# A fused linear-attention and gated feed-forward kernel: last stores split by 64 rows, partial sums moved to another buffer, filler matmuls and a new order

## The chip, the cores and the metric

The kernel runs on one core of a Trainium2 chip. The metric is the device time of one execution in microseconds (us), median of several. A core has five engines that run on their own: TensorE (PE; its weight loads are listed as PEld), VectorE (DVE), ScalarE (ACT), GpSimd (POOL) and SyncE (SP), which here only issues transfers. Sixteen DMA engines move the data. The engines wait for each other through semaphores; each works through its own queue strictly in order.

## The reference

Four batches, eight heads of width 48 and 768 positions go through a linear attention with a decaying state. Its output, 3072 tokens of width 384, goes through a feed-forward layer of width 2048 whose gate is a cosine.

```python
for t in range(S):                      # attention, per batch and head
    cur = outer(u * k[t], v[t])
    y[t] = r[t] @ (state + cur)
    state = w * state + outer(k[t], v[t])
h = x @ w_in                            # x: (3072, 384), w_in: (384, 2048)
g = h * cos(h)
out = g @ w_out                         # w_out: (2048, 384)
```

The weights arrive in double precision. The kernel turns each into a high and a low single-precision part and multiplies three times (high by high, low by high, high by low).

## The kernel before, in words

**Attention.** The 3072 tokens are worked in 24 chunks of 128. The first eight ("early") chunks hold the first positions of each batch. They have to be done before the feed-forward layer can run without breaks. A chunk is loaded (k, r, v), transposed on PE, scaled by the decay on DVE (`rT`, `kT`, L982 and L1001), multiplied (L1065), masked (L1073), and multiplied again into `x` (L1087, L1100), which ACT and DVE split into `xh` and `xl`. The sixteen later chunks do the same in another layout (L1383, L1389, L1463) between the steps of the feed-forward layer.

**Feed-forward.** Six blocks of 512 tokens pass through 16 slices of `w_in` and `w_out`, which makes 96 steps. A step is nine matmuls "h" of 512 columns (L503), an elementwise chain that alternates between ACT and DVE (qi L519, rest L522, cosine L525, gate L1586, high part L1589, low part L1592) and nine matmuls "o" (L516), which add into three PSUM banks. Blocks 0 and 1 take turns: their slices come in the pieces 0 to 2, 2 to 5, 5 to 10 and 10 to 16, since the weights arrive while they work. At the end of each of their first three pieces the three banks are copied to SBUF (L1623) and stored to scratch memory `part_d`: the first piece by SP (L1631), the next two by GpSimd transfers that add to what is there (L1633). At the fourth piece the sums are loaded back (L1641) and added, and DVE turns each bank into the buffer `ot` (L1652), from which SP stores the block in 16 transfers (L1671). There is one `ot` buffer of 128 x 1536 numbers. The copies take a buffer of the ring `R_f`, six buffers of 128 x 512 that also hold the cosine's argument, the converted weights and part of each later chunk.

**The last block** multiplies the other way round (L509), so its four chunks come out with tokens on the partitions. Each is copied (L1702) to a buffer of `R_f` and stored (L1712), the first three by SP, the last one by ACT.

**The order.** Each operation has an entry in `DUES` (a due time) and some an entry in `HOLDS`. A planner in `Plan.one_pass` runs through them with costs (in `op(...)`) and with a time `lat` until a result can be used, picks on each engine what is ready and due first, chooses buffers from the rings and so writes the queues. Buffers and waits follow from that order. Before the first attention product on PE (`first_A`), the planner's gaps on PE are filled with matmuls on zeros (`warm_up`, L1730), one per 0.22 of planned gap.

```python
def st():
    (nc.scalar if last else nc.sync).dma_start(dst, ob())
op(ACT if last else SP, s + 2.5, 0.6, st, [oc], [ob], lat=2.5)
```

Of the kernel before, what the change touches and what calls it, by code (L numbers as in the profile page):

```python
# [9 lines left out]
F32 = mybir.dt.float32  # L10
# [32 lines left out]
    136758, -74847, -43844, -28732, 302616, -88975, -71328, 46773, 176240, 38114, 271897, 215557, 326974,  # L43
    108836, 53012, 131186, -161706, 278206, -84719, -293075, -54461, -7640, 283819, -85697, 225756, 5593,
    -186679, -10247, -73373, -28930, -162082, 217987, -259366, -177497, -84941, -159201, -82184, -80393, -43863,
    -83055, -77972, 11589, -57274, -33785, -170957, -72005, 201058, -45669, 74469, -60635, 116586, -1076,
    111276, 75119, -54793, 79940, -38890, -89278, -125768, -238696, -60653, -52997, 21625, 301534, -101593,
    254771, -262222, -4970, -219414, 28091, -15110, -97894, -118263, 12053, -110128, 63549, 133177, 18614,
    -6951, 60025, -22060, -45024, -49677, 34204, 60125, -200205, -13302, -66174, -33036, -94433, -91164,
    -125037, -46149, -20654, -8595, 24466, -21539, 53811, 138429, 106136, -172876, 50367, -26165, 15995, 24273,  # L50
    -73113, -59577, 52435, -99831, 6426, -50099, 93499, -60680, -32457, -42871, 114144, 77795, 144490, 137391,
    58783, -23367, 58577, 208422, -111209, 186777, -11076, -42885, 38423, 100425, 7413, 63119, 35933, -82873,
    250196, 68613, 170627, 73983, 171298, 116684, 190202, 18014, 349844, 16050, 103196, -271912, -28477, 57946,
    290925, 2146, 33561, 87750, 82736, 172361, 96028, 40836, 105696, -9361, -144107, -33123, 99741, 1720,
    222152, -3585, 44166, 292726, 50264, -3417, 78702, 53863, 549, 113465, 8699, 37860, 176553, 165585, 100038,
    33248, -20572, -128785, 1518, 144259, 60247, 111734, -19349, 32045, 66708, -119633, -62142, 103845, 7872,
    221906, 105376, -223574, 64391, -119475, 99981, -10143, 69206, 82857, 22816, 161156, -2214, 80786, -18511,
    137292, 151469, 17062, -117219, 27894, 24386, 27670, 204170, 162618, 78171, 259079, 174814, 138450, 181046,
    10238, 112906, 347641, 318538, 211144, 102107, 153373, 148521, 132607, 118433, 89292, 171696, 128704,
    224680, 119833, 142656, 216497, 338377, 224213, 228681, 52471, 182421, 269447, -15748, 147984, 302852,  # L60
    286074, 34347, 185044, 298071, 23180, 78723, -179449, 119380, 127630, 4739, 200362, -47882, -78624, -67,
    101807, 208108, 151590, 281102, 33345, -24492, 84778, 189293, 149176, 299002, 138086, 120838, 117666,
    211708, 219288, 158855, 153765, 181158, 156137, 207030, 225525, 219795, 263347, 151158, 256475, 125769,
    109988, 90100, 99225, 182830, 149079, 210335, 235226, 217064, 109197, 158205, 373177, 166519, 231418,
    368046, 231808, 402665, 265446, 135760, 146596, 193207, 92655, 123719, 102006, 230749, 209030, 135713,
    186620, 213224, 193786, 310481, 321361, 240739, 159885, 356326, 109821, 206409, 160655, 36410, 117505,
    88418, 132605, 96715, 156058, 162907, 220231, 298782, 364481, 93736, 17158, 212980, -73432, 288595, 294841,
    296470, 172246, 66723, 372492, 296138, 168690, 134186, 224480, 266863, 261899, 191662, -237199, 374999,
    -8877, 107834, 204368, 189738, 236846, 275244, 395143, 104624, 363087, 387425, 335888, 381053, 217061,
    412705, 377859, 323997, 156149, 261201, 425835, 270672, 337145, 263398, 149282, 222003, 244052, 247831,  # L70
    248047, 247831, 214675, 320956, 240127, 336022, 244681, 246600, 428199, 207444, 245430, 210426, 250803,
    241749, 251901, 251612, 251612, 248581, 253162, 253162, 251012, 251312, 251312, 251962, 252712, 254012,
    258703, 259383, 259740, 261940, 264140, 265440, 267940, 269380, 270240, 267980, 268840, 269340, 270590,
    273560, 274810, 275560, 275560, 271840, 277110, 277110, 274960, 275260, 275260, 275910, 276660, 277960,
    285405, 286085, 271217, 273417, 275617, 276917, 282935, 284375, 285235, 282975, 283835, 280817, 285585,
# [191 lines left out]
    0.8, 1256: 0.1, 1258: 0.2, 1259: 0.8, 1260: 0.8, 1262: 0.8, 1263: 0.3, 1264: 0.2, 1265: 0.3, 1267: 0.5,  # L267
    1268: 0.2, 1269: 0.2, 1270: 0.2, 1272: 0.8, 1273: 0.3, 1274: 0.8, 1275: 0.8, 1277: 0.3, 1278: 0.5, 1280:
    0.2, 1281: 0.2, 1282: 0.3, 1284: 0.1, 1286: 0.2, 1287: 0.3, 1289: 0.2, 1290: 0.2, 1294: 0.5, 1297: 0.8,
    1299: 0.1, 1304: 0.5, 1308: 0.2, 1310: 0.1, 1317: 0.1, 1318: 0.1,  # L270
}


# [1610 lines left out]
```

## Time and profile before

| | us |
|---|---|
| median of 3 runs | 506.78 (506.75 to 508.08) |
| the profiled execution, its own time | 507.42 |
| its span (first to last instruction) | 505.6 |
| PE busy | 475.6 (94%) |
| DVE busy | 370.3 (73%) |
| ACT busy | 292.2 (58%) |
| GpSimd busy | 222.2 (44%) |
| mean granted TensorE clock | 0.981 |

The span is the part of an execution that the rows cover; 1.82 us of the profiled execution lie around it. Matmuls overlap and their ends are modelled, so that a PE that is busy in a whole stretch has no wait in it, and no more can be read from its share.

### The profile page before, as it was taken

What the parts mean: (1) busy time and instruction counts of PE and PEld (TensorE: products, weight loads), DVE (VectorE), ACT (ScalarE), POOL (GpSimd) and SP (SyncE); (2) the same over time, 40 slices, a digit from 0 to 9 for tenths busy, and PEclk for the clock granted to TensorE, in tenths of its full rate; (3) what the DMA queues carried; (4) which work ended last, traced back from release to release, by engine and by line L of the source; (5) the groups of instructions that cost most, each with busy time, mean ns of one, the idle gap of its engine ahead of it and who ended that gap; (6) DMA issues with size and microseconds to landing.
All of it is one profiled execution on the core that took longest, in us unless ns stands there. A gap on an engine that the chain in (4) does not pass through costs nothing.

```text
span 505.6 us, 11867 instructions
## 1 busy us (share of the span) xinstructions
PE 475.6 (94%) x4475; PEld 391.7 (77%) x4475; DVE 370.3 (73%) x686; ACT 292.2 (58%) x652; POOL 222.2 (44%) x225
## 2 busy tenths in 40 slices
PE   7999999999899999999999999999999999999940
PEld 6787788777678887688888888888888888899940
DVE  7899997998978967877787777678677557444430
ACT  5897876786765464465656555556555544444420
POOL 7674357746655874644484541574524200000000
PEclk9899999999999999999999999999999999999985
DMA  8774668869277565676873473766373300200001
GB/s 160 141 177 127 202 178 189 153 170 211 89 171 178 99 129 143 140 167 168 185 180 84 102 176 109 169 137 149 100 164 99 100 1 10 55 1 0 1 26 40
DMA packets 142538, 61.69 MB, mean 122 GB/s; under 512 B 122476, under 2 KB 135308, under 8 KB 142476
## 3 DMA queue, kind: packets, MB, share of 16 engines
q1 hardware_dynamic: 140554, 57.50, 46.4%
q0 software_dynamic: 1728, 3.15, 3.9%
q8 instruction: 36, 0.59, 0.5%
q10 hardware_dynamic: 194, 0.25, 0.1%
q14 instruction: 26, 0.21, 0.1%
HBM read 51.43 MB, written 9.44 MB: 120 GB/s over the span
## 4 chain that ended last, share of the span: by engine, by line
PE 75%; DVE 8%; DMA 5%; SPq 3%; ACT 2%; issue 1%; POOL 1%; DVEq 0%; ACTq 0%; POOLq 0%
PE bank L503 32%; PE bank L516 27%; PE bank L509 7%; PE bank L1383 3%; PE bank L1463 3%; DMA raw<-in_moe_w_out_dram 2%; DMA part<-f 1%; DVE f L864 1%; SPq L1671 1%; PE bank L973 1%; DVE f L876 1%; DVE A L1073 1%; DMA f<-part 1%; PE bank L1100 1%; ACT A L1038 1%
## 5 line engine op out<-in xcount | busy, mean ns | idle before, releaser
L503 PE MATMUL bank<-xh,w_in_hi 128*128 128x512 f32 x288 | 113.7, 395 | 1.8 <-DVE gl L1592 1.8
L503 PE MATMUL bank<-xh,w_in_lo 128*128 128x512 f32 x288 | 112.6, 391 | 1.2 <-DVE w_in_lo L888 1.2
L503 PE MATMUL bank<-xl,w_in_hi 128*128 128x512 f32 x288 | 112.4, 390 | 0.0
L519 ACT ACTIVATE qi<-bank 128x512 int32<-128x512 f32 (+1 forms) x102 | 58.0, 573 | 88.9 <-PE bank L503 83.7
L522 DVE SCALAR_TENSOR_TENSOR f<-bank,qi 128x512 f32<-128x512 f32 (+1 forms) x102 | 66.4, 655 | 58.3 <-ACT qi L519 56.6
L516 PE MATMUL bank<-gh,w_out_hi 128*128 128x512 f32 x240 | 96.0, 400 | 1.6 <-DVE ot L1652 1.1
L516 PE MATMUL bank<-gl,w_out_hi 128*128 128x512 f32 x240 | 93.7, 390 | 0.7 <-DVE gl L1592 0.7
L516 PE MATMUL bank<-gh,w_out_lo 128*128 128x512 f32 x240 | 93.6, 390 | 0.1
L1589 ACT CAST gh<-bank 128x512 fp32r<-128x512 f32 x94 | 54.9, 585 | 39.4 <-PE bank L516 28.5
L525 ACT ACTIVATE f<-f 128x512 f32<-128x512 f32 (+1 forms) x102 | 61.6, 608 | 27.3 <-DVE f L522 26.7
L1592 DVE TENSOR_TENSOR gl<-bank,gh 128x512 fp32r<-128x512 f32 x94 | 64.1, 683 | 16.7 <-ACT gh L1589 15.9
L1586 DVE TENSOR_TENSOR bank<-bank,f 128x512 f32<-128x512 f32 x94 | 65.0, 692 | 11.4 <-ACT f L525 10.8
L503 PEld LDWEIGHTS bank<-xh,w_in_hi 128*128 128x128 f32 x288 | 54.0, 188 | 14.3 <-DVE gl L1592 3.1
L503 PEld LDWEIGHTS bank<-xh,w_in_lo 128*128 128x128 f32 x288 | 54.1, 188 | 13.4 <-DVE w_in_lo L888 1.6
L503 PEld LDWEIGHTS bank<-xl,w_in_hi 128*128 128x128 f32 x288 | 54.1, 188 | 10.7
L885 POOL TENSOR_TENSOR f<-f,raw 128x384 int32<-128x384 int32 x32 | 35.2, 1100 | 46.1 <-DVE f L876 28.0
L516 PEld LDWEIGHTS bank<-gh,w_out_hi 128*128 128x128 f32 x240 | 45.0, 188 | 12.7 <-issue 1.5
L516 PEld LDWEIGHTS bank<-gl,w_out_hi 128*128 128x128 f32 x240 | 45.1, 188 | 10.1 <-DVE gl L1592 1.6
L516 PEld LDWEIGHTS bank<-gh,w_out_lo 128*128 128x128 f32 x240 | 45.1, 188 | 10.0 <-DVE w_out_lo L888 0.6
L1330 POOL TENSOR_TENSOR A<-rT,decT_r 48x512 f32<-48x512 f32 x32 | 41.5, 1298 | 25.4 <-PE bank L1463 17.4
L1364 POOL TENSOR_TENSOR A<-ident,a 64x512 f32<-64x512 f32 x32 | 35.8, 1120 | 15.0 <-DVE a L1356 13.5
L1325 POOL TENSOR_TENSOR kT<-kT,decT_k 112x512 f32<-112x512 f32 x16 | 21.9, 1371 | 45.1 <-DVE kT L1310 38.8
(132 smaller groups left out, 719.0 us busy)
## 6 DMA issues: line engine op xcount, KB each, us to landing
raw<-in_moe_w_in_dram SPq DMA_DIRECT2D x32, 384.0 KB
raw<-in_moe_w_out_dram SPq DMA_DIRECT2D x32, 384.0 KB
raw<-in_k_dram SPq DMA_DIRECT2D x63, 80.0 KB
raw<-in_r_dram SPq DMA_DIRECT2D x63, 80.0 KB
out_dram<-ot SPq DMA_DIRECT2D x80, 48.0 KB
k<-in_k_dram SPq DMA_DIRECT2D x32, 96.0 KB
f<-in_r_dram SPq DMA_DIRECT2D x32, 96.0 KB
vr<-in_v_dram SPq DMA_DIRECT2D x32, 96.0 KB
```

The lines of the kernel that those rows point to most:

```text
L503: nc.tensor.matmul(ph, a, b_, start=(i == 0), stop=(i == len(mm) - 1))
L509: nc.tensor.matmul(acc, a[:, ts], b_[:, f, :], start=(first and i == 0), stop=(last and i == 2))
L516: nc.tensor.matmul(acc, b_[:, f, n * P : (n + 1) * P], a, start=(first and i == 0), stop=(last and i == 2))
L519: nc.scalar.activation(qi, ph, AF.Copy, scale=INV_2PI, bias=0.25)
L522: nc.vector.scalar_tensor_tensor(q, ph, INV_2PI, qi, op0=ALU.mult, op1=ALU.subtract)
L525: nc.scalar.activation(q, q, AF.Sin, scale=TWO_PI, bias=0.5 * math.pi)
L885: return lambda: eng.tensor_tensor(ai(), ai(), cn(), op=ALU.add)
L1330: nc.gpsimd.tensor_tensor(by_batch(plane(ar, j))[rows[j]], by_batch(late_t(rT))[rows[j]], late_d(decT_r)[rows[j]], op=ALU.mult)
L1364: nc.gpsimd.tensor_tensor(plane(ar, j)[side[j]], ident2[side[j], None, :].to_broadcast(to), ab()[side[j], :, None].to_broadcast(to), op=AL ...
L1586: nc.vector.tensor_tensor(g()[:, cs], ph()[:, cs], q()[:, cs], op=ALU.mult)
L1589: nc.scalar.copy(gh()[:, cs], g()[:, cs])
L1592: nc.vector.tensor_tensor(gl()[:, cs], g()[:, cs], f32(gh())[:, cs], op=ALU.subtract)
```

## The change

1. **Last block's stores.** The destination of a chunk was one pattern of 2 batches x 64 rows x 384 numbers. Now each half (64 rows x 384) is a transfer of its own; of the last chunk SP issues the first half and ACT the second.
2. **Partial sums.** They are copied into the thirds of the buffer `ot` (`R_pt`) in place of buffers of `R_f`. The planner counts 4 and 7 us until such a store has landed (2.5 before), and 4 us for the load back.
3. **Filler matmuls.** `warm_up` goes on after the first attention product, one per 0.35 of planned gap, until the first step of the feed-forward layer. In the built program there are 28 of them (18 before), 24 of them ahead of the first attention product. Ahead of the first small product on PE (of the decay, L662) stand 9 (6 before).
4. **Numbers.** The planner's cost of a matmul is a little lower, and all entries of `DUES` and `HOLDS` are new, so that every queue has a new order.

```diff
-        R_ot = [Tile(att.tile([P, TB // G, 3, G], F32, name="ot"))]
+        ot_all = att.tile([P, 3 * TB], F32, name="ot")
+        R_pt = [Tile(ot_all[:, m * TB : (m + 1) * TB]) for m in range(3)]
+        R_ot = [Tile(ot_all.rearrange("q (t n g) -> q t n g", n=3, g=G), R_pt)]
...
-            oh = op(PE, s, 9 * (0.0058 + 0.000437 * w_), h, ...
+            oh = op(PE, s, 9 * (0.0058 + 0.000432 * w_), h, ...
...
-                        ob = Buf(R_f)
+                        ob = Buf(R_pt)
...
-                            SP if f0 == 0 else POOL, s + 2.5, 1.1 if f0 else 0.6, st, [oc, stored.get((n, m))], [ob], lat=2.5
+                            SP if f0 == 0 else POOL, s + 2.5, 1.1 if f0 else 0.6, st, [oc, stored.get((n, m))], [ob], lat=7.0 if f0 else 4.0
...
-                dst = out.rearrange("(b s) n -> b s n", b=B)[2 * m : 2 * m + 2, at : at + CT, :]
+                dst = [out[b * S + at : b * S + at + CT, :] for b in (2 * m, 2 * m + 1)]
...
-                    (nc.scalar if last else nc.sync).dma_start(dst, ob())
-
-                op(ACT if last else SP, s + 2.5, 0.6, st, [oc], [ob], lat=2.5)
+                    for b in range(2):
+                        (nc.scalar if last and b else nc.sync).dma_start(dst[b], ob()[b * CT : (b + 1) * CT])
+
+                op(ACT if last else SP, s + 2.5, 0.6 if last else 1.2, st, [oc], [ob], lat=2.5)
...
-                    n = int(min(o.gap, 6.0) / 0.22)
+                    n = int(min(o.gap, 6.0) / 0.22) if started is None else int(o.gap / 0.35)
...
-                    before = o is not first_A[0]
+                    started = started or (o if o is first_A[0] else None)
+                    before = o.group < 200
...
 DUES = (
-    136758, -74847, -43844, -28732, 302616, -88975, -71328, 46773, 176240, 38114, 271897, 215557, 326974,
```

**The end, on SP.** The last transfers of SP's queue before (L1671 stores a turned block, L1712 a chunk of the last block):

```order
L1671 DMA out_dram<-ot 4x32x96 x16
L1747 TENSOR_LOAD flag
L1747 ISA x2
L1712 DMA out_dram<-f_99 2x64x384
L1712 DMA out_dram<-f_101 2x64x384
L1712 DMA out_dram<-f_102 2x64x384
```

And now (the same lines are L1677 and L1719):

```order
L1677 DMA out_dram<-ot 4x32x96 x16
L1755 TENSOR_LOAD flag
L1755 ISA x2
L1719 DMA out_dram<-f_101 64x384 x2
L1719 DMA out_dram<-f_102 64x384 x2
L1719 DMA out_dram<-f_100 64x384 x2
L1719 DMA out_dram<-f_97 64x384
```

Three transfers of 2x64x384 became seven of 64x384; the eighth half is issued by ACT, as the fourth chunk was.

**The start, on DVE.** DVE's queue from the decay table on, before (L982 scales the transposed r, L1001 the transposed k, L988 and L993 multiply k by r and by the decay, L1029 sums, L1073 masks):

```order
L686 TENSOR_TENSOR pq<-pq 128x4x2
L694 TENSOR_TENSOR decT_r<-pq,pe 128x512
L982 TENSOR_TENSOR rT_91<-bank,decT_r 112x512
L988 TENSOR_TENSOR f_97<-vr,k_85 128x384
L1001 TENSOR_TENSOR kT_89<-bank,decT_k 112x512
L982 TENSOR_TENSOR rT_92<-bank,decT_r 112x512
L1029 TENSOR_REDUCE a_128<-f_97 128x8
L993 TENSOR_TENSOR k_85<-k_85,dec_k 128x8x48
L993 TENSOR_TENSOR k_86<-k_86,dec_k 128x8x48
L1001 TENSOR_TENSOR kT_90<-bank,decT_k 112x512
L1073 COPY_PREDICATED A<-upper,bank 128x512
```

And now (lines are 6 higher):

```order
L700 TENSOR_TENSOR decT_r<-pq,pe 128x512
L692 TENSOR_TENSOR pq<-pq 128x4x2
L988 TENSOR_TENSOR rT_91<-bank,decT_r 112x512
L994 TENSOR_TENSOR f_97<-vr,k_85 128x384
L1007 TENSOR_TENSOR kT_90<-bank,decT_k 112x512
L1007 TENSOR_TENSOR kT_89<-bank,decT_k 112x512
L1035 TENSOR_REDUCE a_128<-f_97 128x8
L999 TENSOR_TENSOR k_85<-k_85,dec_k 128x8x48
L988 TENSOR_TENSOR rT_92<-bank,decT_r 112x512
L1079 COPY_PREDICATED A<-upper,bank 128x512
```

The second chunk's `kT_90` moved from behind both multiplications of k to ahead of them, and the second of these (`k_86`) moved behind the first masks. On GpSimd, eight clearings of k and v buffers now stand ahead of the identity matrix that PE's first product reads.

**Block 0's stores, on SP.** A stretch of SP's queue around the loads of block 1's partial sums (`part_0_82`, `part_1_83`, `part_2_84`), before; four stores of block 0 stand above it:

```order
L1255 DMA vr<-in_v_dram 64x8x48 x2
L1266 DMA raw_110<-in_k_dram 32x8x80 x4
L1641 DMA f_101<-part_0_82 128x512
L1641 DMA f_100<-part_2_84 128x512
L1266 DMA raw_111<-in_r_dram 32x8x80 x4
L1641 DMA f_102<-part_1_83 128x512
L1671 DMA out_dram<-ot 4x32x96 x12
L1255 DMA k_86<-in_k_dram 64x8x48 x2
```

And now:

```order
L1677 DMA out_dram<-ot 4x32x96 x4
L1272 DMA raw_110<-in_k_dram 32x8x80 x4
L1272 DMA raw_111<-in_r_dram 32x8x80 x4
L1677 DMA out_dram<-ot 4x32x96 x4
L1647 DMA f_99<-part_0_82 128x512
L1647 DMA f_98<-part_2_84 128x512
L1261 DMA k_85<-in_k_dram 64x8x48 x2
L1677 DMA out_dram<-ot 4x32x96 x4
L1261 DMA f_102<-in_r_dram 64x8x48 x2
L1261 DMA vr<-in_v_dram 64x8x48 x2
L1677 DMA out_dram<-ot 4x32x96 x4
L1647 DMA f_97<-part_1_83 128x512
```

All 16 stores of block 0 now stand ahead of the last load of block 1's partial sums; before, twelve stood behind it.

## Rows read from the trace of the kernel before

**Rows 1.** Windows: busy us (instructions) per engine, granted clock, DMA share, GB/s.

```profile
5.00:45.00 40.00, 36.57 (x685) 30.65 (x686) 36.49 (x70) 34.02 (x99) 26.75 (x31) 0.96 0.73 164
85.00:205.00 120.00, 113.80 (x1076) 90.21 (x1074) 101.42 (x173) 72.95 (x151) 74.32 (x70) 1.00 0.66 149
205.00:486.50 281.50, 281.45 (x2507) 235.50 (x2506) 193.58 (x364) 151.45 (x338) 97.11 (x87) 1.00 0.42 102
486.50:505.60 19.10, 0.03 (x1) 0.00 (x0) 0.56 (x1) 0.02 (x1) 0.00 (x0) 0.59 0.12 41
```

**Rows 2.** Timeline, end: start us, us, engine, line, operation; brackets: idle before, releaser.

```profile
484.52 2.75 SPq L1712 DMA_DIRECT2D out_dram<-f  x3
486.19 0.34 PE L509 MATMUL bank<-w_out_lo,gh 128*128 128x384 f32 x1
486.57 0.56 DVE L1702 COPY f<-bank 128x384 f32<-128x384 f32 x1 [1.01 <-PE bank L509]
487.16 0.64 ACTq L1712 DMA_DIRECT2D out_dram<-f  x1
```

**Rows 3.** Windows, inside the end.

```profile
496.00:497.00 1.00, 0.00 (x0) 0.00 (x0) 0.00 (x0) 0.00 (x0) 0.00 (x0) 0.50 0.13 49
...
503.00:504.00 1.00, 0.00 (x0) 0.00 (x0) 0.00 (x0) 0.00 (x0) 0.00 (x0) 0.50 0.02 9
```

**Rows 4.** Timeline, two issues of SP on otherwise quiet queues.

```profile
357.67 1.29 SPq L1255 DMA_DIRECT2D vr<-in_v_dram  x2
392.76 0.42 SPq L774 DMA_DIRECT2D raw<-in_moe_w_out_dram  x1
```

**Rows 5.** Windows, behind these two issues.

```profile
358.50:359.00 0.50, 0.50 (x4) 0.41 (x3) 0.50 (x2) 0.00 (x0) 0.34 (x1) 1.00 0.00 0
359.00:359.50 0.50, 0.50 (x3) 0.40 (x3) 0.50 (x1) 0.00 (x0) 0.50 (x1) 1.00 0.66 119
...
395.50:396.00 0.50, 0.50 (x4) 0.42 (x3) 0.50 (x2) 0.48 (x2) 0.00 (x0) 1.00 1.00 395
```

**Rows 6.** Timeline, the start on PE and GpSimd.

```profile
1.23 1.46 PE L1730 MATMUL bank<-warm 128*128 128x256 bf16 x6 [1.23 <-DVE pq L626]
2.62 0.38 PE L662 MATMUL bank<-ident,wr 8*64 8x4 f32 x4
1.43 0.49 POOL L602 MEMSET k<- 128x128 f32 x3
1.86 0.80 POOL L602 MEMSET vr<- 128x128 f32 x5
11.41 1.67 PE L1065 MATMUL bank<-rT,kT 48*128 48x128 f32 x16 [1.32 <-DVE kT L1001]
```

**Rows 7.** Waits of DVE, 5 to 45 us: us in total, times, longest.

```profile
DVE rT L982 <- PE bank L973: 1.2, 3, 0.9
DVE A L1073 <- ACT A L1038: 1.0, 3, 0.4
```

**Rows 8.** Timeline, a stall that begins with a partial sum's store.

```profile
147.61 0.36 DVE L864 TENSOR_SCALAR f<-raw 128x384 int32<-128x384 int32 x1 [1.17 <-DMA part<-f]
148.49 0.50 PE L503 MATMUL bank<-xh,w_in_lo 128*128 128x512 f32 x1 [1.22 <-DVE w_in_lo L888]
```

**Rows 9.** Timeline, block 0's last stores and PE behind them.

```profile
191.39 8.03 SPq L1671 DMA_DIRECT2D out_dram<-ot  x12
200.69 0.50 PE L503 MATMUL bank<-xh,w_in_hi 128*128 128x512 f32 x1 [0.85 <-DVE gl L1592]
204.15 0.47 PE L516 MATMUL bank<-gh,w_out_hi 128*128 128x512 f32 x1 [1.14 <-DVE ot L1652]
```

**Rows 10.** Instructions of the tile part: its adding stores' time to landing.

```profile
DMA to landing us min/median/max: 4.0/6.2/8.4
```

**Rows 11.** Timeline, an adding store and the next copy into the same third.

```profile
88.28 0.88 POOL L1633 DMA_DIRECT2D part<-f  x1
93.26 0.58 ACT L1623 COPY f<-bank 128x512 f32<-128x512 f32 x1
```

More of the change, by code (lines that the diff above doesn't have):

```diff
@@ L1557, in h @@
                 mm_h(ph()[:, 0 : nt * C], xh[:, j : j + nt], xl[:, j : j + nt], f)
-            oh = op(PE, s, 9 * (0.0058 + 0.000437 * w_), h, [*x_ready[n], w_ready[2 * f]], [ph, *xs], lat=0.3, line="h")
+            oh = op(PE, s, 9 * (0.0058 + 0.000432 * w_), h, [*x_ready[n], w_ready[2 * f]], [ph, *xs], lat=0.3, line="h")
             if s in look:
@@ L1614, in add_t @@
                     oo = op(
-                        PE, s + 3.0 + 0.01 * m, 3 * (0.0058 + 0.000437 * w_), o, [gs_[s][0], w_ready[2 * f + 1]], [acc[m], gh, gl], lat=0.3, line="o"
+                        PE, s + 3.0 + 0.01 * m, 3 * (0.0058 + 0.000432 * w_), o, [gs_[s][0], w_ready[2 * f + 1]], [acc[m], gh, gl], lat=0.3, line="o"
                     )
@@ L1640, in add_t @@
                         pb = Buf(R_f)
-                        ol = op(SP, s - 1.0, 0.6, lambda: nc.sync.dma_start(pb(), part_d[n][m]), [stored[n, m], oh], [pb], lat=2.5)
+                        ol = op(SP, s - 1.0, 0.6, lambda: nc.sync.dma_start(pb(), part_d[n][m]), [stored[n, m], oh], [pb], lat=4.0)
                         oo = op(
@@ L1732 @@
         order = plan.order()
-        before = True
+        before, started = True, None
         with tc.manual_schedule():
```

455 rows, old and new, of tables (DUES, HOLDS) are left out of this document.

## Prediction

> **What bounds the kernel now.** I read the busy time of the engines in a few long stretches first [rows 1]. From 205 us to 486.5 us PE has no idle time (281.45 of 281.50 us), so that stretch is as long as its matmuls, and the change leaves their number alone. Idle time of PE is found in three places: about 3.4 us of the 40 us from 5 to 45, where DVE (36.5) and ACT (34.0) are nearly as full as PE, 6.2 us of the 120 us from 85 to 205, and all of the last 19.1 us. The last stretch is the largest by far, and no engine works in it.
>
> Next the timeline of the end [rows 2]. PE's last matmul ends at 486.5, the last copy out of PSUM at 487.1, and ACT issues the last store at 487.16. The span ends at 505.6. What fills the rest is shown by one-microsecond windows [rows 3]: the DMA engines are busy to 0.13, which is 2.1 of 16, and move 49 GB/s until they run dry just behind 503. The four stores hold 4 x 128 x 384 x 4 bytes = 786 KB, and 786 KB at 49 GB/s take 16.0 us. So the end waits for four transfers that run on two DMA engines, and the outermost dimension of their destination is 2.
>
> Last I read who was waited for where PE stops in the middle: a load of weights waited for a store of partial sums [rows 8], and the turned block waited for the one before it to be stored [rows 9].
>
> **The last stores.** A transfer is now 64 rows of 1536 bytes. How such a one spreads, the trace shows twice, from two sides. Loads of 64 x 8 pieces of 192 bytes, issued at 357.67 on a quiet queue [rows 4], move nothing until 359.0 and then 119 GB/s at a share of 0.66, some ten engines [rows 5]; so the first byte comes 1.3 us after the issue begins. Weight loads of 128 rows that lie end to end in memory, the last of them issued at 392.76, run at 395 GB/s and a share of 1.00. Rows of 1536 bytes are nearer to the second. Then the transfers no longer bound the end, and their issue does: SP issues seven of them from 484.52 on at about 0.64 us each (ACT's price for one [rows 2]), and the last starts at 484.52 + 6 x 0.64 = 488.4. First byte at 489.7, 98 KB at 395 GB/s in 0.25 us, so the data are out at 490.0. From the last bytes at 503.2 to the end of the span there are 2.4 us now, and I keep them: 492.4. **The term is 505.6 - 492.4 = 13.2 us saved.** Bounds: if all 786 KB go at 119 GB/s from 484.52 + 1.3 on, they end at 492.4 and the span at 494.8, which saves 10.8. If an issue of SP costs the 0.42 of the weight load, seven are through by 487.5, and ACT's issue at 487.16 decides: 487.16 + 1.3 + 0.25 + 2.4 = 491.1, which saves 14.5.
>
> A rule of the Trainium skill speaks against such a split. "DMA: Bandwidth & Descriptors", section "Rules for kernel authors", says that two transfers to disjoint halves of the partitions are not worth it, since both spread over the same 16 engines and take turns. By that rule this term would be nothing. The Trainium skill's same page ("DMA: Bandwidth & Descriptors"), section "Why a DMA increments its semaphore by 16 and not by 1", says that the number of engines is the largest up to 16 that divides the slowest dimension of both sides, which gives 2 now and 16 after; the share of 0.13 agrees with it, so that the premise of the first rule (all 16 used already) doesn't hold here.
>
> **The start.** PE's first product that matters (L662, from which all decay tables come) stands behind six filler matmuls, which run from 1.23 to 2.62 us [rows 6], 0.23 us each. With nine it starts 0.7 us later, and DVE's tables with it. The clearings that now precede the identity matrix ran from 1.43 to 2.66 us on GpSimd, behind it; put ahead of it, they make it ready near 2.7 at the latest, which the nine fillers cover up to 3.3. Without the three more fillers the product would be 0.1 us late for that reason alone. Against that stands the order on DVE. PE waited 1.32 us for `kT_90` at 11.41 us, which now stands ahead of two multiplications. DVE's own waits for PE and ACT in this stretch add up to 2.2 us in these rows [rows 7], and its instructions are the same. If none of them goes, the start is 0.7 us worse; if all go, it is 1.5 us better. The first kind (for PE's transposed r, 1.2 us) is behind the late `kT_90`; the second (for ACT's diagonals) has nothing that speaks for its going. I take 0.7 - 1.2: **0.5 us saved**. The fillers behind the first product stand in planned gaps and are priced at nothing: PE waits there for DVE. Where such a gap is gone, one costs 0.23 us at most.
>
> **Partial sums in the buffer of the turned sums.** At 147.61 DVE had waited 1.17 us for an adding store that held a buffer of `R_f`, and PE then stood 1.22 us until the low part of the weights was ready [rows 8]. With the copies out of `R_f` this wait can't be there: **1.2 us saved**. What is late next: the third of `ot` is free only when the last store from it has landed. Adding stores land 4.0 to 8.4 us after their issue, 6.2 in the middle [rows 10]. In the tightest place one was issued at 88.28 and the next copy into the same third stood at 93.26 [rows 11]. 88.28 + 6.2 = 94.5, so ACT would wait 1.2 us, and behind it in ACT's queue stand the elementwise chains of the running steps, for which PE waits. At 8.4 us it is 3.4 us, at 4.0 nothing. I charge the middle in full: **1.2 us lost**. The plain stores of the first piece and the turning itself come many microseconds after the last use.
>
> **Block 0's stores.** Twelve of them were issued from 191.39 to 199.4, behind loads, and block 1's turning and PE stood behind them for 0.85 and 1.14 us [rows 9]. All now stand ahead of the load that the turning needs anyway. **2.0 us saved**; nothing if SP is held up at an earlier load, since its queue is in order.
>
> The other 3 us of PE's waits from 85 to 205 us (6.2 - 1.2 - 2.0) come from weights that are late and from DVE and GpSimd in each other's way. Their places move with the new order; I leave them as they are, with all gone (3 us better) and as much again (3 us worse) as bounds.
>
> **The sum.** 13.2 + 0.5 + 1.2 - 1.2 + 2.0 = 15.7 us. For the profiled execution: span 505.6 - 15.7 = 489.9, and with the 1.82 us around it 491.7 in place of 507.42. The median of the runs shown lies 0.64 us below that execution, so the median goes from 506.78 to 491.1; I say 491.
>
> **The rivals.** *The middle gives nothing back.* The stores spread, but new waits take the place of the old: ACT behind adding stores (3.4 us at worst), new late weights (3 us), and a start that is 0.7 us later. For it: ACT's queue is in order, and every queue has a new order that no trace has shown. Against: the planner now counts 7 us for an adding store, nearer to 6.2 than its 2.5 before. With only the end's term 493.6, with all of this and the old waits 500.7.
>
> *All waits in the middle go.* Then 13.2 + 1.5 + 6.2 = 20.9 us, 486. Against it: the waits for weights have causes that the change doesn't touch.
>
> *The halves take turns.* Both halves of a chunk share engines, so that together they take what the whole took, and the end stays at its 16 us of transfer. Then only the 2.5 us of the other terms are left: 504.3. Against it stand the 64-row loads with ten engines busy. The Trainium skill's rule on two halves, quoted above, would have it so.
>
> *Slower: one run, one engine.* The half's destination is one unbroken run of 98 KB in memory. If a transfer to such a run goes through a single DMA engine, 786 KB move at half of 49 GB/s, in 32 us, 16 us longer than now: 506.8 + 16 - 2.5 = 520. It decides as soon as fewer than two engines work. Against it: the weight loads also read unbroken memory and fill all 16.
>
> **Chances.** My forecast, between 487.5 and 493, has 0.68; the first rival, 493 to 497 for the most part, 0.20, with 0.02 beyond; the full gain 0.06; the halves in turn 0.02; the single engine 0.02. From 487 to 497 lie nearly nine in ten of these; the end's bounds (10.8 to 14.5) fit in. Some 0.3% (1.5 us) is what a measurement of this kernel can tell from no change. By the same cases: faster 0.97, same 0.01, slower 0.02.
>
> **What would show it.** The stretch from PE's last matmul to the end of the span should be about 6 us in place of 19.1, with a DMA share far above 0.13 in it. The wait of DVE for `part` should be gone, as should PE's waits near 200 us. PE's L662 product should start near 3.3 us, and the first feed-forward matmuls no later than now. The copies of partial sums on ACT may show waits for DMA. I am wrong if the share at the end stays near two engines, or if ACT's waits for adding stores reappear as waits of PE for several microseconds.

## The result, and the profile after

The changed kernel takes 490.04 us (median of 4 runs, 488.78 to 490.70); the kernel before took 506.76 beside it. The ratio is 0.966, with an interval of 0.964 to 0.969. The forecast was 491.0, with 487 to 497 as its range. The profiled execution of the changed kernel took 488.78 us, its span is 487.1.

The windows of the changed kernel, cut at its own end of PE's work, answer to [rows 1]:

```profile
5.00:45.00 40.00, 39.26 (x718) 32.14 (x717) 37.17 (x76) 33.91 (x99) 27.65 (x32) 1.00 0.74 166
85.00:205.00 120.00, 118.90 (x1039) 94.65 (x1039) 106.57 (x179) 76.69 (x158) 73.95 (x69) 1.00 0.67 152
205.00:480.10 275.10, 275.10 (x2538) 230.08 (x2536) 187.31 (x355) 147.14 (x330) 96.65 (x87) 1.00 0.42 103
480.10:487.10 7.00, 0.00 (x0) 0.00 (x0) 0.56 (x1) 0.00 (x0) 0.00 (x0) 0.83 0.39 102
```

All four rows moved. The last was 19.1 us long and is 7.0. PE's idle time from 85 to 205 us was 6.2 us and is 1.1. From 5 to 45 us it was 3.4 and is 0.7, and the granted clock there rose from 0.96 to 1.00; but fillers count as busy, and most of that fall is theirs (see "Fewer fillers"). The third stretch ends earlier; it still has no gap.

The end of the changed kernel in its timeline, beside [rows 2], and then single microseconds of it, beside [rows 3] (DMA share and GB/s are the last two columns):

```profile
478.08 5.01 SPq L1719 DMA_DIRECT2D out_dram<-f  x7
...
479.76 0.34 PE L513 MATMUL bank<-w_out_lo,gh 128*128 128x384 f32 x1
480.14 0.56 DVE L1708 COPY f<-bank 128x384 f32<-128x384 f32 x1 [1.01 <-PE bank L513]
480.73 0.55 ACTq L1719 DMA_DIRECT2D out_dram<-f  x1
```

```profile
482.00:483.00 1.00, 0.00 (x0) 0.00 (x0) 0.00 (x0) 0.00 (x0) 0.00 (x0) 1.00 0.92 242
484.00:485.00 1.00, 0.00 (x0) 0.00 (x0) 0.00 (x0) 0.00 (x0) 0.00 (x0) 0.86 0.22 59
```

The DMA engines now fill to 0.92 where the share was 0.13. SP issues seven transfers with no pause above 0.11 us between them, until 483.09, which is 3.0 us behind PE's last matmul (it ends at 479.76 + 0.34 = 480.10). The view of this line gives the shortest, the middle and the longest issue in ns, and the start of the first and of the last:

```profile
L1719 SPq DMA_DIRECT2D out_dram<-f x7: 534/572/1200, 478.1 to 482.5; - x7
```

Six of the seven take 0.53 to 0.60 us; the second takes 1.20.

Every wait of PE that the timeline of the changed kernel shows behind 20 us:

```profile
40.15 0.51 PE L507 MATMUL bank<-xh,w_in_lo 128*128 128x512 f32 x1 [0.36 <-DVE w_in_lo L894]
86.69 0.50 PE L520 MATMUL bank<-gl,w_out_hi 128*128 128x512 f32 x1 [0.22 <-DVE gl L1598]
89.31 0.50 PE L507 MATMUL bank<-xh,w_in_lo 128*128 128x512 f32 x1 [0.15 <-DVE w_in_lo L894]
174.43 0.27 PE L1389 MATMUL bank<-A,kT 48*64 48x64 f32 x1 [0.32 <-POOL A L1336]
```

The waits of [rows 8] and [rows 9] are not among them. To split the 18.5 us by which the span is shorter, I use one more mark in each timeline: the first of the feed-forward matmuls that run on without a pause. It is this row in the kernel before, and the second in the changed kernel:

```profile
45.69 0.50 PE L503 MATMUL bank<-xh,w_in_hi 128*128 128x512 f32 x1
```

```profile
44.28 0.50 PE L507 MATMUL bank<-xh,w_in_hi 128*128 128x512 f32 x1
```

The start is then 45.69 - 44.28 = 1.4 us shorter. From this mark to the end of PE's last matmul it was 440.8 us and is 480.10 - 44.28 = 435.8, so 5.0 shorter. The tail is 12.1 us shorter (19.1 to 7.0).

### The profile page after: what moved, and what is told of

Read it like the earlier page. It is cut to its first block, busy times and chain, and to the rows that moved or that the text cites. A ratio compares the mean times of both kernels' runs of the same rounds, so it can differ in the third digit from the quotient of the medians.

```text
span 487.1 us, 11851 instructions
## 1 busy us (share of the span) xinstructions
PE 477.0 (98%) x4485; PEld 392.2 (81%) x4485; DVE 369.0 (76%) x686; ACT 291.7 (60%) x652; POOL 221.0 (45%) x225
## 4 chain that ended last, share of the span: by engine, by line
PE 75%; DVE 9%; DMA 6%; POOL 4%; issue 3%; ACT 2%; SPq 0%; POOLq 0%; DVEq 0%; ACTq 0%
PE bank L507 33%; PE bank L520 26%; PE bank L513 7%; PE bank L1389 3%; PE bank L1469 3%; DMA raw<-in_moe_w_in_dram 3%; DMA raw<-in_moe_w_out_dram 1%; DVE f L882 1%; POOL f L891 1%; PE bank L979 1%; POOL A L1336 1%; DVE A L1079 1%; DMA f<-part 1%; PE bank L1106 1%; PE bank L1737 1%
## 5 line engine op out<-in xcount | busy, mean ns | idle before, releaser
L507 PEld LDWEIGHTS bank<-xh,w_in_hi 128*128 128x128 f32 x288 | 54.1, 188 | 12.1 <-DVE gl L1598 0.6
L1370 POOL TENSOR_TENSOR A<-ident,a 64x512 f32<-64x512 f32 x32 | 34.7, 1084 | 18.2 <-DVE a L1362 16.7
```

The source lines that it names most:

```text
L507: nc.tensor.matmul(ph, a, b_, start=(i == 0), stop=(i == len(mm) - 1))
L1370: nc.gpsimd.tensor_tensor(plane(ar, j)[side[j]], ident2[side[j], None, :].to_broadcast(to), ab()[side[j], :, None].to_broadcast(to), op=AL ...
```

## The experiments

The theory behind the first group: a transfer uses few DMA engines when its destination has an outermost dimension of 2, so the tail is a matter of the transfers' shape; two halves that take turns are the main rival. For the second group: the start and the middle come from due times and buffer, by the terms of the prediction. All ratios are to the kernel before, run beside each.

**The split alone**, in the kernel before.

```diff
-dst = out.rearrange("(b s) n -> b s n", b=B)[2 * m : 2 * m + 2, at : at + CT, :]
+dst = [out[b * S + at : b * S + at + CT, :] for b in (2 * m, 2 * m + 1)]
...
-(nc.scalar if last else nc.sync).dma_start(dst, ob())
+for b in range(2):
+    (nc.scalar if last and b else nc.sync).dma_start(dst[b], ob()[b * CT : (b + 1) * CT])
```

> The kernel before with nothing changed but the last block's stores, two transfers of 64 rows for each chunk. Theory (what a transfer can use depends on the outermost dimension of its destination, 2 before and 64 now): the stretch from PE's last matmul to the end of the span falls from 19.1 to about 7.0 us, as in the changed kernel, and the time from 506.8 to about 494.7 us; the middle and the start stay as they were. Rival (the halves take turns): the tail stays at 19 us, the time at 506.8. If the 5 us that the middle gained also came from the stores (they can't, they are the last instructions), the time would be about 490.

It took 495.78 us (493.49 to 497.91), ratio 0.977 (0.973 to 0.981). The tail of the profiled execution, from the end of PE's last matmul on:

```profile
487.82:495.20 7.38, 0.00 (x0) 0.00 (x0) 0.56 (x1) 0.00 (x0) 0.00 (x0) 0.83 0.39 98
```

7.4 us at 98 GB/s in place of 19.1: the split brings about 11 to 12 us by itself, and the halves do not take turns. The time lies 1.1 us above the 494.7 of the theory; in the profile the start was longer, with the mark at 47.32 in place of 45.69. More on that below.

**The whole chunk again**, in the changed kernel, with `dst` as it was before.

```diff
-for b in range(2):
-    (nc.scalar if last and b else nc.sync).dma_start(dst[b], ob()[b * CT : (b + 1) * CT])
+(nc.scalar if last else nc.sync).dma_start(dst, ob())
```

> The changed kernel with the last block's chunks stored as one transfer again. Theory: the DMA share of the tail falls back to about 0.13 at 49 GB/s, the tail from 7.0 to about 19.1 us, the time from 490.0 to about 502. Rival (the new order of the end, not the split, shortened the tail): the tail stays near 7 us and the time near 490.

502.03 us (500.87 to 503.47), ratio 0.991 (0.987 to 0.994). Its tail:

```profile
480.33:499.40 19.07, 0.00 (x0) 0.00 (x0) 0.56 (x1) 0.00 (x0) 0.00 (x0) 0.55 0.12 41
```

The tail is back to 19.1 us, and the time is 12.0 us above the 490.0 of the changed kernel. The new order of the end has no share in it that these profiles show.

**Two halves by columns.** Is it the shape, or that there are twice as many transfers? In the changed kernel, with `dst` as it was before:

```diff
 for b in range(2):
-    (nc.scalar if last and b else nc.sync).dma_start(dst[b], ob()[b * CT : (b + 1) * CT])
+    h = slice(b * DM // 2, (b + 1) * DM // 2)
+    (nc.scalar if last and b else nc.sync).dma_start(dst[:, :, h], ob()[:, h])
```

> The changed kernel, still with two transfers for each chunk and the same queues, but each has all 128 rows and half of the columns (192), so that the outermost dimension of the destination is 2 again. Theory (the shape counts): few engines work again, the share of the tail is 0.13 to 0.25, and the time is 498 to 503 us (498 if the two transfers of a chunk fall on different engines, 502 or more if on the same). Rival (the number of transfers counts, two in flight where one was): as the changed kernel, 490, since there are as many.

503.04 us (501.41 to 503.33), ratio 0.992 (0.989 to 0.995). Its tail, and a microsecond of it:

```profile
480.57:500.60 20.03, 0.00 (x0) 0.00 (x0) 0.56 (x1) 0.00 (x0) 0.00 (x0) 0.58 0.12 39
```

```profile
490.00:491.00 1.00, 0.00 (x0) 0.00 (x0) 0.00 (x0) 0.00 (x0) 0.00 (x0) 0.50 0.14 46
```

Eight transfers as in the changed kernel, and a tail of 20.0 us. So it is not the number of transfers; the shape with an outermost dimension of 2 is slow either way. In every microsecond from 481 to 498 the share is 0.12 to 0.17, although ACT's transfer stands in a queue of its own beside SP's seven: transfers of one queue and of two shared about two engines, as the dearer branch of the expectation had it. The Trainium skill, "DMA: Bandwidth & Descriptors", section "Why a DMA increments its semaphore by 16 and not by 1", says that a transfer issued from SP or ACT takes the lowest-numbered engines; the trace fits this, but it shows only how many engines work and not which.

The kernel before also holds a shape in between. The stores of a turned block (4x32x96) run alone from 427 us on, and two microseconds of them read:

```profile
433.00:435.00 2.00, 2.00 (x13) 1.86 (x12) 1.39 (x4) 1.24 (x3) 0.00 (x0) 1.00 0.31 72
```

A share of 0.31 is five of 16 engines, with an outermost dimension of 4: more than with 2, and far from the 0.92 with 64. These stores go out in pieces of 384 bytes, so it is not unbroken memory alone that brings in more engines.

**Both queues.** SP issues the first half of each chunk, ACT the second.

```diff
-(nc.scalar if last and b else nc.sync).dma_start(dst[b], ob()[b * CT : (b + 1) * CT])
+(nc.scalar if b else nc.sync).dma_start(dst[b], ob()[b * CT : (b + 1) * CT])
```

> The changed kernel, with the second half of every chunk issued by ACT and the first by SP (before, SP issued seven of the eight). Theory (the issue on SP bounds the tail: its last issue ends at 483.09, 2.4 us behind the last copy): both last halves are issued at about 480.7, the data are out 1.7 us earlier, the time is about 488.3. Rival (the transfers themselves or what follows them bound the tail): 490.0, or 490.5 if ACT's issues delay its last copy.

489.00 us (487.37 to 490.28), ratio 0.965 (0.961 to 0.968); the changed kernel had 0.966. PE ends at 480.21 and the span at 486.7: a tail of 6.5 us, 0.5 less, where 1.7 was expected. The issues did move: the last that SP makes is through at 480.70 + 1.10 = 481.8 and ACT's at 480.70 + 1.37 = 482.07, where it was 483.09. But bytes flow for longer behind the last issue:

```profile
480.70 1.37 ACTq L1719 DMA_DIRECT2D out_dram<-f  x2
...
480.70 1.10 SPq L1719 DMA_DIRECT2D out_dram<-f  x2
```

```profile
483.00:483.50 0.50, 0.00 (x0) 0.00 (x0) 0.00 (x0) 0.00 (x0) 0.00 (x0) 0.50 0.69 204
483.50:484.00 0.50, 0.00 (x0) 0.00 (x0) 0.00 (x0) 0.00 (x0) 0.00 (x0) 0.50 0.05 15
484.00:484.50 0.50, 0.00 (x0) 0.00 (x0) 0.00 (x0) 0.00 (x0) 0.00 (x0) 0.50 0.07 16
```

The first fence is the timeline, the second half microseconds of the end. From 483.5 on, about one engine of 16 still works. So with issue out of the way the transfers decide: that is read from this one trace. The Trainium skill, "Perfetto Trace Analysis", section "DMA Optimizations", says that spreading issues over the engines that can issue may help where issuing is the limit; here it helps by 0.5 us in the trace, and the change of the time lies within the intervals. Two profiles of the changed kernel itself differ by 0.2 us in the tail (7.0 and 7.2).

**Half the rows.**

```diff
-(nc.scalar if last and b else nc.sync).dma_start(dst[b], ob()[b * CT : (b + 1) * CT])
+(nc.scalar if last and b else nc.sync).dma_start(dst[b][0 : CT // 2], ob()[b * CT : b * CT + CT // 2])
```

> The changed kernel, but each of the last block's transfers has only the first 32 of its 64 rows, so that half of that block's rows is left out of the output; as many issues on the same queues, half the bytes. What is left to settle: two queues saved only 0.5 us of the tail in the trace where 1.7 were expected. Theory (with issues out of the way the transfers themselves bound the tail): the tail falls from 7.0 to about 6 us or less, the time to about 489. Rival (the seven issues of SP bound it): the tail stays at 6.8 to 7.0, the time at 489.5 to 490, unless an issue of 32 rows is cheaper than the 0.71 us of one of 64.

489.49 us (488.24 to 491.66), ratio 0.964 (0.961 to 0.967). PE ends at 481.45, the span at 488.1: a tail of 6.65 us. Half the bytes save 0.35 us of 7.0.

```profile
L1719 SPq DMA_DIRECT2D out_dram<-f x7: 355/419/1730, 479.4 to 483.6; - x7
```

Of the 0.35 us, 0.3 are SP's own: its last issue starts 2.1 us behind PE's end, where it was 2.4. That is nearer to the rival: as the change stands, SP's issues bound its tail. The gain is hardly more than the 0.2 us by which two profiles of one kernel differ, so this is the better reading and not a proof.

**Quarters.** Four transfers of 32 rows for each chunk.

```diff
-for b in range(2):
-    (nc.scalar if last and b else nc.sync).dma_start(dst[b], ob()[b * CT : (b + 1) * CT])
+for b in range(4):
+    r = slice(b % 2 * CT // 2, b % 2 * CT // 2 + CT // 2)
+    (nc.scalar if last and b > 1 else nc.sync).dma_start(dst[b // 2][r], ob()[b * CT // 2 : (b + 1) * CT // 2])
```

> The changed kernel with four transfers of 32 rows for each chunk: the same bytes and shape, twice the issues (14 on SP). Theory (an issue costs the same whatever its rows, 0.71 us): SP issues until about 488, the tail is 11 to 12 us, the time 494 to 495. Rival (the cost of an issue goes with its rows, so that 14 cost what 7 did): as the changed kernel, 490.

491.88 us (491.43 to 493.72), ratio 0.969 (0.967 to 0.972). PE ends at 480.95, the span at 490.2: a tail of 9.25 us, 2.25 longer, where 4 to 5 were expected.

```profile
478.92 7.95 SPq L1720 DMA_DIRECT2D out_dram<-f  x14
...
L1720 SPq DMA_DIRECT2D out_dram<-f x14: 322/419/1347, 478.9 to 486.5; - x14
```

14 issues take 7.95 us where seven took 5.01. The middle one takes 0.42 us, as in the experiment before, where one of 64 rows takes 0.57; the second is again a long one (1.35). A mean (7.95 / 14 = 0.57, 5.01 / 7 = 0.72) mixes it in. Neither expectation holds as it was put: half the rows make an issue cheaper, but by a quarter and not by half, so splitting further costs more than it brings.

**Buffer without due times.** The copies go to the thirds of `ot`, while the order of all instructions stays that of before. This is in the kernel with the split alone, and the plan still sets a buffer of `R_f` aside. Not printed here are the definition of `R_pt`, which is as in the change, and the same edit in the plain store.

```diff
...
-return lambda: copy(ob(), acc[m]())
+return lambda: copy(R_pt[m].ap, acc[m]())
...
-nc.gpsimd.dma_start(part_d[n][m], ob(), accum_op=ALU.add)
+nc.gpsimd.dma_start(part_d[n][m], R_pt[m].ap, accum_op=ALU.add)
```

> The kernel of the first experiment (before, with the last stores split) and the copies of partial sums written to the thirds of the buffer ot; every instruction of every engine stands where it stood, since the plan still sets a buffer of R_f aside for each. So it differs from the changed kernel by the due times, the clearings and the fillers alone. Theory A (the prediction's two terms, -1.2 for the wait of DVE that goes and +1.2 for copies that wait on ACT): as the first experiment, 495.8 us. Theory B (the wait goes and no copy on ACT costs anything): 494.6. Theory C (the buffer gave the whole 5 us of the middle): 490.8. In A and B the waits of PE for late weights and for the last stores of block 0 (107, 127 to 130, 200 and 204 us) stay; in C they are gone.

493.94 us (491.19 to 495.85), ratio 0.975 (0.971 to 0.979), beside 0.977 of the split alone. The medians alone cannot tell B from A. The trace can: from the mark (47.87) to PE's end (486.54) it is 438.7 us, where the kernel before had 440.8 and the split alone 440.5. DVE's wait for a store of `part` and PE's wait of 1.22 us behind it are gone. ACT's copies wait for a store once, 0.7 us, and no wait of PE follows from it. Behind 100 us PE has four waits. Those at 200 and 204 us stay, as in A and B. Those near 107 and from 127 to 130 are gone; the two at 122 and 128 are new and belong to earlier steps (counted by `gl`, the 17th and 18th, where the wait of 0.92 us in the kernel before is for the 19th):

```profile
122.28 0.50 PE L503 MATMUL bank<-xh,w_in_hi 128*128 128x512 f32 x1 [0.91 <-DVE gl L1594]
128.68 0.50 PE L503 MATMUL bank<-xh,w_in_hi 128*128 128x512 f32 x1 [1.31 <-DVE gl L1594]
...
200.93 0.50 PE L503 MATMUL bank<-xh,w_in_hi 128*128 128x512 f32 x1 [0.63 <-DVE gl L1594]
204.13 0.47 PE L516 MATMUL bank<-gh,w_out_hi 128*128 128x512 f32 x1 [0.85 <-DVE ot L1654]
```

So theory C falls. By itself the buffer brings 1 to 2 of the 5.0 us of the middle: 438.7 against 440.5 us, and PE's idle time from 85 to 205 us is 4.4 us here and 5.4 with the split alone. The rest came only with the new due times on top.

**Due times without buffer.** The other way about, in the changed kernel, for partial sums.

```diff
-ob = Buf(R_pt)
+ob = Buf(R_f)
```

> The changed kernel with the copies of partial sums back in the buffers of R_f. The plan has fewer of these buffers at hand then and puts some instructions elsewhere, so this is the changed kernel's due times without the buffer that they were made for. Theory (the due times, not the buffer, gave most of the middle): only a wait like that of 1.2 us for an adding store comes back, 491.2. Rival (due times and buffer belong together): several waits of PE come back between 85 and 205 us, 493 to 495.

503.54 us (501.85 to 504.83), ratio 0.991 (0.988 to 0.994): 13 us slower than the changed kernel, and far beyond both expectations. From the mark (45.02) to PE's end (495.73) it is 450.7 us, 10 more than in the kernel before. Two of its ten waits of PE from 85 to 215 us, and a stretch in which the clock fell:

```profile
89.42 0.80 PE L520 MATMUL bank<-gl,w_out_hi 128*128 128x512 f32 x1 [1.91 <-DVE gl L1598]
...
144.33 0.50 PE L520 MATMUL bank<-gh,w_out_hi 128*128 128x512 f32 x1 [1.97 <-ACT f L1629]
```

```profile
89.00:95.00 6.00, 5.58 (x72) 4.34 (x73) 3.98 (x8) 2.76 (x6) 3.76 (x4) 0.50 0.27 31
```

With the buffer short, the plan sends instructions elsewhere, and these due times, made for one set of buffers, are worse on another than the old ones (495.78 us with the split alone). At 144.33 PE waits for a copy of partial sums itself. As the order changes with the buffer, this does not price the due times; it shows that the two edits belong together.

**Fewer fillers.** Those behind the nineteenth are left out.

```diff
+fill = []
...
-if n:
+n = min(n, 19 - sum(fill))
+if n > 0:
+    fill.append(n)
     warm_up(n)
```

> The changed kernel without its filler matmuls behind the nineteenth (from 7.57 us on; 9 of them are left out). Theory (the fillers keep PE's clock up): PE is idle for much of 8.5 to 11 us, the granted clock is 0.5 for about three microseconds soon after, as it was in the kernel before from 11.95 us on, and the first feed-forward matmuls come about 1.4 us later: 491.4. Rival (fillers in gaps are worth nothing, as the prediction priced them): the clock stays at 1.00, the time at 490.0.

488.49 us (486.99 to 491.36), ratio 0.966 (0.961 to 0.970), beside 489.45 of the changed kernel in the same set. The granted clock stays at 1.00 from 5 to 15 us, though PE is idle for 1.5 us there (0.72 in its longest wait), and the mark is at 44.03. The theory falls: these fillers are worth nothing that can be measured, as the prediction priced them. From 5 to 45 us PE is idle for 2.4 us without them and for 0.7 with them, and the start is no longer for it. So 1.7 of the 2.7 us by which PE's idle time fell there is fillers in the gaps, not waits that went.

**Six fillers first.**

```diff
+fill = []
...
-if n:
+n = min(n, 6) if not fill else n
+if n > 0:
+    fill.append(n)
     warm_up(n)
```

> The changed kernel with six fillers ahead of the first product, as before, in place of nine. Theory (the three cost 0.23 us each, as the prediction charged): the first product starts near 2.6 to 2.8 us in place of 3.26, DVE's tables with it, and the time is 489.4. Rival (the three fillers also keep the clock, or something else than this product is late next): 490.0 or above.

488.72 us (488.25 to 490.16), ratio 0.966 (0.962 to 0.970). The first product starts at 2.67 us in place of 3.26, so 0.6 us earlier, and the mark is at 44.04 in place of 44.28 (44.68 in the second profile of the changed kernel, next). The median lies 0.7 below that of the changed kernel, well inside the intervals: not settled.

**The changed kernel again**, with no edit.

> The changed kernel itself once more, as the measure for the three that run beside it: 490.0 us, PE's last matmul at about 480.1, with the same few waits.

489.45 us (488.38 to 491.33), ratio 0.966 (0.963 to 0.970). Its profiled execution was a long one, 491.33 us: PE's last matmul ended at 482.40, from the mark (44.68) to there it is 437.7 us, 1.9 more than in the first profile. A difference below 2 us in one stretch of one profile therefore proves little, and I read the 1 to 2 us of the buffer above as rough. The gain of the middle as a whole stands: in the ten profiles with the new due times and `R_pt` the stretch is 435.4 to 437.7 us long, in the two with neither it is 440.8 and 440.5.

**Two small gains together.** Six fillers first, and the halves issued by SP and ACT in turn.

```diff
...
+n = min(n, 6) if not fill else n
...
-(nc.scalar if last and b else nc.sync).dma_start(dst[b], ob()[b * CT : (b + 1) * CT])
+(nc.scalar if b else nc.sync).dma_start(dst[b], ob()[b * CT : (b + 1) * CT])
```

> The changed kernel with the two edits that each came out some tenths of a microsecond shorter: six fillers ahead of the first product, and the last block's halves issued by SP and ACT in turn. If both gains add up (0.7 for the start by the first product's 3.26 to 2.6 us, 0.5 for the tail): 488.8 us. If neither is real: 490.0.

488.12 us (487.04 to 488.32), ratio 0.961 (0.958 to 0.963). This is the fastest of all; its interval meets that of the changed kernel (0.963 to 0.970 in the repeated run) only at its edge. PE ends at 479.86, the span at 486.6. The changed kernel itself did not run beside it, and its profile shows neither gain clearly: the mark is at 44.47 (44.28 and 44.68 in the two profiles of the changed kernel), the tail is 6.75 us (7.0 and 7.2). That it is 1 us or more faster is likely, not shown.

## Why the prediction was right, step by step

**The last stores** were to save 13.2 us and saved 12.1. The mechanism was right: shape, not number, and then the issue on SP. The tail came out 1.1 us longer than forecast by two terms. From PE's end to the start of SP's last issue I had 1.9 us (6 issues at 0.64); it is 2.4, because the second of the six took 1.20 us, while the others took less than I charged. Why it did stays open. From there to the last byte I had 1.55; bytes flow until 484.6, 2.1 us. From the last byte to the end of the span it is 2.5. I kept 2.4 from the kernel before; in finer windows its last bytes move just ahead of 503.4, which leaves 2.2. I had taken the rate from a load (395 GB/s, share 1.00 [rows 5]); these stores reach 242 GB/s at a share of 0.92, less for each busy engine.

The rule of the Trainium skill against two halves ("DMA: Bandwidth & Descriptors", section "Rules for kernel authors") does not hold here, by 11 to 12 us in two experiments. It presumes that the one transfer uses all engines.

**The start** was to save 0.5 us and saved 1.4 in this pair of profiles. As charged, the three fillers moved the first product from 2.62 to 3.26 us; that the start became longer by as much is not shown (with six fillers the mark was at 44.04). What I did not see is the clock. From 5 to 15 us the windows of before and after are these:

```profile
5.00:15.00 10.00, 7.88 (x96) 6.60 (x97) 8.70 (x15) 6.63 (x20) 7.89 (x10) 0.85 0.70 139
```

```profile
5.00:15.00 10.00, 9.62 (x133) 7.93 (x132) 9.13 (x18) 6.54 (x20) 7.01 (x9) 1.00 0.81 158
```

In the kernel before, the granted clock was 0.50 (the lower of its two levels) for 3.4 us there. In the split alone, which has the same order of instructions, it was 0.50 for twice as long:

```profile
11.90:15.31 3.41, 3.41 (x44) 2.71 (x44) 2.42 (x7) 2.81 (x9) 3.33 (x4) 0.50 0.19 38
```

```profile
11.42:18.25 6.83, 6.83 (x74) 5.71 (x75) 4.63 (x9) 2.91 (x9) 5.10 (x6) 0.50 0.53 103
```

PE was busy throughout. By an estimate from these rows, half the clock cost half of each stretch: 1.7 us in the kernel before, 3.4 in the split alone. That is what their marks differ by (45.69 and 47.32), and without it both marks would lie near 44.0. The old order with the new buffer fits too: 6.8 us at 0.50 and the mark at 47.87. The ten profiles with the new due times and `R_pt` have a clock of 1.00 from 5 to 15 us and the mark at 44.0 to 44.9. By this estimate the clock accounts for the whole gain of the start, 1.7 to 3.4 us in the three profiles with the old order.

The step that failed is the one that counted only waits (0.7 - 1.2) and left out the clock. The 1.2 was DVE's wait for PE's transposed r; it did not go, it fell by 0.3:

```profile
DVE rT L988 <- PE bank L979: 0.9, 2, 0.7
```

That 0.5 us was forecast and a gain of the same sign came is luck. What brought the clock down is argued, not shown: in the three profiles with the old order PE was idle for 2.1 to 2.3 us from 5 to 15 us, most of it just before `kT_90` (1.32 us, [rows 6]), and the clock fell right behind; in the ten with the new order it was idle for 0.1 to 1.5, and the clock held. No experiment changed this wait alone. That the fillers prevent the fall was my next theory, and it fell.

**Partial sums and block 0's stores** were to give 1.2 - 1.2 + 2.0. The wait of DVE is gone, as the buffer alone also showed, and the 1.2 us that I charged for copies behind adding stores did not come: stores land after 4.0 to 8.0 us as before, yet no copy on ACT waits for one. Both waits of [rows 9] are gone. Together that is 3.2 of the 5.0 us, with the charge of 1.2 mis-sized: it is nothing.

**The other 3 us of waits**, which I left as they are, went for the larger part: PE's idle time from 85 to 205 us fell from 6.2 to 1.1 us, and 5.1 - 3.2 = 1.9 of that is theirs. This step failed, in the safe direction. I had put them down to late weights and engines in each other's way and taken their cause as untouched. One candidate is DVE's waits for DMA from 85 to 205 us. In the kernel before they were, in us, times and longest:

```profile
DVE rT L1310 <- DMA raw<-in_r_dram: 2.3, 1, 2.3
DVE ot L1652 <- DMA f<-in_r_dram: 2.1, 1, 2.1
DVE f L864 <- DMA raw<-in_moe_w_out_dram: 2.0, 2, 1.4
DVE kT L1310 <- DMA raw<-in_k_dram: 1.5, 1, 1.5
DVE f L522 <- DMA part<-f: 1.3, 1, 1.3
DVE bank L1646 <- DMA f<-part: 1.3, 1, 1.3
DVE f L864 <- DMA part<-f: 1.2, 1, 1.2
```

They sum to 11.7 us. In the changed kernel the same view has these:

```profile
DVE ot L1658 <- DMA out_dram<-ot: 0.5, 1, 0.5
...
DVE f L870 <- DMA raw<-in_moe_w_in_dram: 0.2, 1, 0.2
...
DVE f L870 <- DMA raw<-in_moe_w_out_dram: 0.2, 1, 0.2
```

0.9 us in all. DVE is busy for 101 of these 120 us in the kernel before and for 107 in the changed one, so it has little room, and its queue is in order. One place in the kernel before shows the whole chain, on DVE and then on PE:

```profile
127.41 0.36 DVE L864 TENSOR_SCALAR f<-raw 128x384 int32<-128x384 int32 x1 [1.43 <-DMA raw<-in_moe_w_out_dram]
127.80 1.25 DVE L876 SCALAR_TENSOR_TENSOR f<-raw,f 128x384 int32<-128x384 int32 x1
128.97 0.68 DVE L1592 TENSOR_TENSOR gl<-bank,gh 128x512 fp32r<-128x512 f32 x1
```

```profile
129.71 0.50 PE L503 MATMUL bank<-xh,w_in_hi 128*128 128x512 f32 x1 [0.92 <-DVE gl L1592]
```

A conversion of weights waits 1.43 us for its load, `gl` stands behind it, and PE waits 0.92 us for `gl`. With the buffer alone this wait of DVE is gone, but PE waits 1.31 us for the `gl` of the step before (at 128.68, above). There ACT waits for a load of weights, and DVE, ahead of that `gl`, for ACT:

```profile
125.64 0.54 ACT L858 ACTIVATE raw<-raw 128x384 int32<-128x384 uint32 x1 [1.61 <-DMA raw<-in_moe_w_in_dram]
```

```profile
126.74 0.70 DVE L1588 TENSOR_TENSOR bank<-bank,f 128x512 f32<-128x512 f32 x1 [1.90 <-ACT f L525]
```

So a late load reaches PE through whichever engine stands at it, and the sum on DVE alone does not set PE's idle time. In the changed kernel ACT's waits for DMA in these 120 us went up from 2.0 to 6.5 us, and DVE's waits for the other engines from 5.6 to about 11. With the due times but without the buffer DVE waits only this long for DMA, and PE is idle for 9.7 us:

```profile
DVE f L870 <- DMA raw<-in_moe_w_out_dram: 1.2, 2, 0.9
...
DVE f L870 <- DMA raw<-in_moe_w_in_dram: 0.6, 1, 0.6
```

What the runs show is that these waits went with the new due times and the buffer together; by which of the moved instructions, and whether through DVE's loads, stays open, since buffers, due times and the planner's costs change together.

**The rivals.** "All waits in the middle go" was nearest to what the middle did, and I gave it 0.06; with the tail at its real 12.1 us it comes to 487 and not to 486. The shortfall of the tail (1.1) and the surplus of start and middle (0.9 + 3.0) leave 2.8 us, which is what the span came out shorter than forecast (487.1 for 489.9). The median of 490.0 lies 1.0 below the forecast. That it is so near is partly luck: errors of 1.1 us one way and 3.9 the other offset each other in part, and the profiled execution was the shortest of its four, 1.3 us below their median, where I had reckoned with one 0.6 above.

## What to carry to other kernels

At the end of a kernel look at the DMA share: if it stands near 2 of 16 engines, read the outermost dimension of both sides of the transfer, and cut along that dimension and not along another; then stop once the issues on the queue take as long as the bytes, since each further issue cost 0.4 to 0.6 us here. When PE waits for an engine whose queue is almost full, read what that engine waits for, and what stands behind that in turn, before calling the wait untouched. Where PE stands idle for long, read the granted clock behind it too: a count of waits leaves out what half the clock costs. Idle time that fillers cover is not time won. Due times that were made for one set of buffers are not to be judged, or used, without it.

## What the runs showed of the hardware beyond that

Two transfers of half the columns, both with an outermost dimension of 2, shared two engines (a share of 0.14) rather than taking four. The middle issue of 32 rows of 1536 bytes on SP takes 0.42 us where one of 64 rows takes 0.57. In all eleven profiles with such halves one of SP's issues, the second in ten of them and the third in one, takes 0.9 to 1.7 us; with whole chunks none takes more than 0.72. Why is open. In one execution of the experiment with due times alone, PE, which stood 1.91 us at once and was idle for most of 87 to 89 us, ran at half clock from 89 to 95 us while it was busy for 5.58 of these 6 us.
